# Attention pieces between expert steps: transposes together, scores with states, one run of outputs

## The chip, the cores and the metric

The kernel runs on one core of one Trainium2 chip. The metric is the device time in microseconds (us) of one execution, taken as the median of several runs. The engines are PE (TensorE, matmuls), DVE (VectorE), ACT (ScalarE), POOL (GpSimd) and SP (SyncE, which here only issues DMAs).

## What is computed

A linear attention with a complex, decaying state feeds a mixture of eight experts whose gate is balanced by eight rounds of row and column normalization. Cut to what matters:

```python
# q, k, v, a_re, a_im: (4, 8, 768, 48)
for t in range(S):
    S_re, S_im = ar * S_re - ai * S_im, ar * S_im + ai * S_re   # a, scaled to |a| <= 0.999
    S_re = S_re + k[:, :, t] (outer) v[:, :, t]
    y[:, :, t] = q[:, :, t] @ S_re
x = y as (3072, 384)
P = exp(x @ w_gate - max); eight times: rows to 1, columns to N / E
for e in range(8):
    out += P[:, e:e+1] * (relu(x @ w1[e]) @ w2[e])
```

## The kernel before

The kernel has two phases. Phase 1 computes the attention and, between its parts, the first two experts. Phase 2 computes the other six experts for all tokens and is not touched.

Phase 1 cuts the 3072 tokens into 12 blocks of 256 (`SUB`), three for each of the four sequences, and each block into two chunks of 128 (`CH`). For a block, `elem(i)` (line 295) makes the cumulative products of `a` and from them scaled keys `kh` and queries `z`, almost all on DVE; this is called the chain of the block here. `mix(i)` (line 427) is the attention proper. It is a generator: what stands between two `yield`s is a piece. For each chunk it issues 12 DMAs on SP that copy keys and queries by heads into `ks` and `qs` (lines 437 to 441; two buffers of each, taken in turn by chunk), and then uses four helpers, each for a half `g` of the eight heads:

- `keys(g)`: four PE transposes of `ks` (L460) and an ACT copy to `kt` (L462)
- `scores(g)`: four PE products of `ks` and `qs` (L474; fp32 products show as two instructions each) and a masked copy on DVE into `sc` (L477)
- `state(g)`: four PE products of `kt` and `v` into `U` (L469)
- `outs(g)`: 16 or 32 small PE products into `xp` (L491), of masked scores with `v` and, unless the chunk is the first of its sequence, of `qs` with the state of the chunk before

The last chunk of a sequence has no keys and no states. After a chunk's states the state is carried on by five DVE operations (L517 to L528). After the outputs, `xh` (L530, ACT) and `xl` (L531, DVE) split the result into a high and a low part for the experts. The transposes and the scores share one PSUM pool of two buffers (tag `s`), `U` and `xp` have one buffer each, and `kt` and `sc` have two.

An expert step (`experts`, line 147) for one of the 16 hidden tiles of the two experts runs six PE matmuls of the second layer for a tile three steps back (L158 to L160) and nine of the first layer (L179 to L181), then two ACT operations and one on DVE (`hl`, L187). A plain step is these 15 matmuls.

For block 0, `phase1` (line 190) runs the pieces of `mix(0)` one after another and after each calls twice the loader of the last weight tiles (`load_thirds`, line 132). For each later block `i` it runs the 16 steps of block `i - 1` and, from step `LEAD` on (11 for block 1, 10, 8, 6 for blocks 2 to 4, then 4), one piece of `mix(i)` after each; the pieces that are left then run in a row.

PE's order is that of the program text (`manual_schedule`). The orders of DVE, ACT and SP are laid out by a planner that simulates the program with a model of the durations; on the chip each engine then follows its order. Three places in it are pinned: `behind` holds both masks of block 0's second chunk and the first mask of block 1 behind certain operations of the next chain.

Before, a chunk has five pieces: transposes and scores of half 0; states of half 0 and transposes of half 1; outputs of half 0 and scores of half 1; states of half 1; outputs of half 1 with all that follows them.

Of the kernel before, what the change touches and what calls it, by code (L numbers as in the profile page):

```python
# [20 lines left out]
NCH = SUB // CH  # L21
# [22 lines left out]
def slot(h):  # L44
    return (h % 4) * 128 + (h // 4) * 80


def piece(h, b):
    q = (h % 4) * 128
    if h < 4:  # L50
        return slice(q + 32 * b, q + 32 * b + 32)
    return slice(q + 96 - 32 * b, q + 128 - 32 * b)


class Net:
# [134 lines left out]
    def phase1(self, c1, ca):  # L190
# [41 lines left out]
        for i in range(ns):  # L232
            mix = self.mix(i)
            if i == 0:
                n = 0
                while True:
                    with tc.issue_after(self.act0.ins), tc.issue_after(self.dve0.ins):
                        if next(mix, self) is self:
                            break
                    with tc.issue_after(self.act0.ins):  # L240
                        for _ in range(2):
                            if late and next(late[0], self) is self:
                                late.pop(0)
                                next(late[0], None) if late else None
                    n += 1
                for g in late:
                    for _ in g:
                        pass
                with tc.issue_after(self.gl.ins):
                    self.elem(1)  # L250
                self.behind(0, 1, 0, k=1)
                self.behind(0, 1, 1, k=3)
                continue
            lg = self.logits(i - 1)
            for n in range(2 * NF):
                self.moe.send((i - 1, n // NF, n % NF))
                if n in (1, 2):
                    next(lg)
                if n >= LEAD.get(i, 4):
                    next(mix, None)  # L260
# [166 lines left out]
    def mix(self, i):  # L427
# [6 lines left out]
        for c in range(NCH):  # L434
# [17 lines left out]
            def keys(g, i=i, c=c, ks=ks, kts=kts, lastc=lastc):  # L452
                if lastc:
                    return
                if i == 0:
                    kt_p = self.psB.tile([128, 4, SK], F32, tag="po", name=f"ktp{i}_{c}_{g}")
                else:
                    kt_p = self.psS.tile([128, 4, SK], F32, tag="s", name=f"ktp{i}_{c}_{g}")
                for j in range(4):
                    nc.tensor.transpose(kt_p[:, j, :], ks[:, 4 * g + j, :], self.ident[:SK, :SK])  # L460
                kts[g] = tmp.tile([128, 4, SK], F32, tag="kt", name=f"kt{i}_{c}_{g}", bufs=2)
                self.kt = nc.scalar.activation(kts[g], kt_p, AF.Copy)  # L462

            def state(g, c=c, U=U, kts=kts, lastc=lastc):
                if lastc:
                    return
                for j in range(4):
                    h = 4 * g + j
                    nc.tensor.matmul(U[:, h, :], kts[g][:, j, :], vt[:, c, slot(h):slot(h) + D], start=True, stop=True)  # L469

            def scores(g, i=i, c=c, ks=ks, qs=qs, sss=sss):
                sp = self.psS.tile([128, 4, CH], F32, tag="s", name=f"sp{i}_{c}_{g}")
                for j in range(4):
                    nc.tensor.matmul(sp[:, j, :], ks[:, 4 * g + j, :], qs[:, 4 * g + j, :CH], start=True, stop=True)  # L474
                ss = sss[g] = self.sc[self.isc]
                self.isc = 1 - self.isc
                self.masks[i, c, g] = nc.vector.copy_predicated(ss, self.mask, sp)  # L477

            def outs(g, c=c, xp=xp, qs=qs, sss=sss, S0=S0, first=first):
                for b in range(2):  # L480
                    for inter in range(1 if first else 2):
                        for j in range(4):
                            h = 4 * g + j
                            q = 32 * j
                            o = xp[q:q + 32, 2 if b else g, :]
                            pc = piece(h, b)
                            lw = S0[:, pc] if inter else vt[:, c, pc]
                            rw = qs[:, h, :CH] if inter else sss[g][:, j, :]
                            st = g == 0 and b == 0 and inter == 0
                            sp_ = g == 1 and b == 1 and (first or inter == 1)  # L490
                            nc.tensor.matmul(o, lw, rw, start=st, stop=sp_, tile_position=(0, q), skip_group_check=True)  # L491

            keys(0)
            scores(0)
            yield
            state(0)
            keys(1)
            yield
            outs(0)
            scores(1)  # L500
            yield
            state(1)
            if not lastc:
                with self.tc.issue_after(self.kt.ins):
                    nc.scalar.activation(rr[0:D], R[0:D], AF.Copy)
                    nc.scalar.activation(rr[64:64 + D], R[0:D], AF.Copy)
                    nc.scalar.activation(rn[0:D], R[64:64 + D], AF.Copy, scale=-1.0)
            yield
            outs(1)
            if not lastc:  # L510
                sh = [SK, 2, H // 2, D]
# [20 lines left out]
            if c == NCH - 1:  # L532
                for a, t in ((0, xh), (1, xl)):
                    nc.sync.dma_start(self.x_d[i // NS][:, i % NS, a], t.bitcast(F32).rearrange("p c (j t) -> p c j t", t=CH))
            yield

    def logits(self, i):
        nc = self.nc
# [483 lines left out]
```

## Time and profile before

| what | us |
|---|---|
| median of 3 runs (1840.32 to 1843.8) | 1842.44 |
| span of the profiled execution | 1839.6 |
| PE busy in the span | 1774.3 |
| DVE busy | 1361.8 |
| ACT busy | 734.3 |
| PE busy from 0 to 92 us (block 0 and the first steps) | 68.95 |
| PE busy from 92 to 308 us (216 us) | 196.31 |
| DVE busy from 92 to 308 us | 191.22 |
| PE busy from 617 to 1839 us (1222 us, after the attention) | 1200.08 |

The span runs from the first to the last instruction of the profiled execution. The page gives no other time of that execution; the runs were timed apart. PE's matmuls overlap, so the busy time of a group is more than the time by which it moves what follows; for that, the starts of matmuls one after the other are read. "Idle before" and "waited for" tell what released an engine after it stood still. The granted clock is the share of full speed at which TensorE ran.

### The profile page before, as it was taken

What the parts mean: (1) busy time and instruction counts of PE and PEld (TensorE: products, weight loads), DVE (VectorE), ACT (ScalarE), POOL (GpSimd) and SP (SyncE); (2) the same over time, 40 slices, a digit from 0 to 9 for tenths busy, and PEclk for the clock granted to TensorE, in tenths of its full rate; (3) what the DMA queues carried; (4) which work ended last, traced back from release to release, by engine and by line L of the source; (5) the groups of instructions that cost most, each with busy time, mean ns of one, the idle gap of its engine ahead of it and who ended that gap; (6) DMA issues with size and microseconds to landing.
All of it is one profiled execution on the core that took longest, in us unless ns stands there. A gap on an engine that the chain in (4) does not pass through costs nothing.

```text
span 1839.6 us, 30590 instructions
## 1 busy us (share of the span) xinstructions
PE 1774.3 (96%) x12024; PEld 1731.9 (94%) x12024; DVE 1361.8 (74%) x3060; ACT 734.3 (40%) x1597; POOL 6.4 (0%) x15
## 2 busy tenths in 40 slices
PE   5979999999999999999999999999999999999998
PEld 3869999999999989899999999998999999999998
DVE  7888989888883586967676767687776767575754
ACT  7534444445443443424242424343433333242421
POOL 1000000000000000000000000000000000000000
PEclk9979999999999999999999999999999999999999
DMA  6333433333332430401010101123220101020100
GB/s 209 96 104 88 132 113 110 116 111 111 118 97 73 147 112 4 150 20 52 18 52 18 52 18 52 49 96 97 69 86 18 52 5 65 1 69 1 52 24 31
DMA packets 120632, 132.83 MB, mean 72 GB/s; under 512 B 9632, under 2 KB 100512, under 8 KB 120480
## 3 DMA queue, kind: packets, MB, share of 16 engines
q1 hardware_dynamic: 119680, 130.41, 23.0%
q8 instruction: 96, 1.57, 0.4%
q14 instruction: 56, 0.46, 0.1%
q10 hardware_dynamic: 800, 0.39, 0.1%
HBM read 88.22 MB, written 23.59 MB: 61 GB/s over the span
## 4 chain that ended last, share of the span: by engine, by line
PE 82%; DVE 9%; DMA 4%; ACT 2%; issue 1%; SPq 1%; DVEq 0%; ACTq 0%
PE po L747 10%; PE po L745 10%; PE po L746 10%; PE P L784 9%; PE P L785 9%; PE P L786 9%; PE po L158 3%; PE ph L180 3%; PE ph L181 3%; PE ph L179 3%; PE po L160 3%; PE po L159 3%; PE sp L474 2%; PE y L491 2%; DMA raw<-in_w_dram 2%; PE U L469 1%
## 5 line engine op out<-in xcount | busy, mean ns | idle before, releaser
L747 PE MATMUL po<-wc,hl 128*128 128x384 f32 x1152 | 385.3, 334 | 3.1 <-DVE hl L806 3.1
L745 PE MATMUL po<-wc,hh 128*128 128x384 f32 x1152 | 385.0, 334 | 0.0
L746 PE MATMUL po<-wc,hh 128*128 128x384 f32 x1152 | 384.8, 334 | 0.0
L805 ACT ACTIVATE hh<-c 128x384 fp32r<-128x384 f32 x384 | 200.9, 524 | 322.2 <-DVE c L794 320.9
L806 DVE SCALAR_TENSOR_TENSOR hl<-c,hh 128x384 fp32r<-128x384 f32 x384 | 211.9, 552 | 66.5 <-ACT hh L805 58.5
L747 PEld LDWEIGHTS po<-wc,hl 128*128 128x128 f32 x1152 | 216.2, 188 | 4.4 <-DVE hl L806 4.4
L745 PEld LDWEIGHTS po<-wc,hh 128*128 128x128 f32 x1152 | 216.2, 188 | 0.4 <-ACT hh L805 0.4
L746 PEld LDWEIGHTS po<-wc,hh 128*128 128x128 f32 x1152 | 216.2, 188 | 0.0
L799 ACT ACTIVATE s<-P 128x384 f32<-128x384 f32 x192 | 94.1, 490 | 270.8 <-PE P L786 270.8
L185 ACT ACTIVATE hh<-ph 128x256 fp32r<-128x256 f32 x192 | 73.3, 382 | 243.7 <-PE ph L181 243.0
L180 PE MATMUL ph<-xl,w 128*128 128x256 f32 x576 | 162.8, 283 | 5.4 <-DVE xl L531 5.4
L179 PE MATMUL ph<-xh,w 128*128 128x256 f32 x576 | 162.2, 282 | 0.6 <-ACT xh L530 0.6
L181 PE MATMUL ph<-xh,w 128*128 128x256 f32 x576 | 162.4, 282 | 0.0
L784 PE MATMUL P<-B,wa 128*128 128x384 f32 x480 | 160.7, 335 | 0.9 <-DVE c L794 0.6
L786 PE MATMUL P<-B,wa 128*128 128x384 f32 x480 | 160.4, 334 | 0.0
L785 PE MATMUL P<-B,wa 128*128 128x384 f32 x480 | 160.4, 334 | 0.0
L158 PE MATMUL po<-w,hh 128*128 128x384 f32 x384 | 141.2, 368 | 1.2 <-ACT yst L163 1.2
L160 PE MATMUL po<-w,hl 128*128 128x384 f32 x384 | 130.7, 340 | 0.0
L159 PE MATMUL po<-w,hh 128*128 128x384 f32 x384 | 130.3, 339 | 0.0
L794 DVE TENSOR_TENSOR c<-P,u 128x384 f32<-128x384 f32 x192 | 106.2, 553 | 31.2 <-PE P L786 29.9
L794 DVE TENSOR_TENSOR u<-u,s 128x384 f32<-128x384 f32 x96 | 53.3, 555 | 100.9 <-ACT s L799 100.9
L187 DVE TENSOR_TENSOR hl<-hf,hh 128x256 fp32r<-128x256 f32 x192 | 80.4, 419 | 48.1 <-ACT hf L186 47.3
(188 smaller groups left out, 3665.4 us busy)
## 6 DMA issues: line engine op xcount, KB each, us to landing
raw<-in_w_dram SPq DMA_DIRECT2D x48, 768.0 KB, 4.3
qs<-z SPq DMA_DIRECT2D x144, 64.5 KB, 2.6
qk<-in_aqk_dram SPq DMA_DIRECT2D x12, 768.0 KB, 4.9
ks<-kh SPq DMA_DIRECT2D x144, 64.0 KB, 2.6
ye_d<-yst SPq DMA_DIRECT2D x48, 192.0 KB, 2.1
y<-ye_d SPq DMA_DIRECT2D x48, 192.0 KB, 2.4
z<-in_aqk_dram SPq DMA_DIRECT2D x11, 768.0 KB, 7.0
B<-x_d SPq DMA_DIRECT2D x40, 192.0 KB, 3.6
```

Source lines behind the costliest of these rows:

```text
L158: nc.tensor.matmul(po[k], hh[:, s], w2h, start=f == 0, stop=False)
L179: nc.tensor.matmul(ph, w[:, 0, cs], xh[:, ct, :], start=(ct == 0), stop=False)
L180: nc.tensor.matmul(ph, w[:, 0, cs], xl[:, ct, :], start=False, stop=False)
L181: nc.tensor.matmul(ph, w[:, 1, cs], xh[:, ct, :], start=False, stop=(ct == NCT - 1))
L745: nc.tensor.matmul(po[k], hh[:, s], w2[:, 0, i], start=first, stop=False)
L746: nc.tensor.matmul(po[k], hh[:, s], w2[:, 1, i], start=False, stop=False)
L747: nc.tensor.matmul(po[k], hl[:, s], w2[:, 0, i], start=False, stop=last)
L784: nc.tensor.matmul(ps, t[:, 0, k], x[:, 0], start=first, stop=False)
L785: nc.tensor.matmul(ps, t[:, 0, k], x[:, 1], start=False, stop=False)
L786: nc.tensor.matmul(ps, t[:, 1, k], x[:, 0], start=False, stop=last)
L805: A.activation(hh, c, AF.Relu)
L806: V.scalar_tensor_tensor(hl, c, 0.0, hh.bitcast(F32), ALU.max, ALU.subtract)
```

## The change

The same helpers are called in another grouping. A chunk's pieces are now: both halves' transposes; both halves' scores, then both halves' states; an empty piece (not for block 0); both halves' outputs with all that follows. In blocks after the first, no `yield` stands after the first chunk's outputs, so the second chunk's copies and transposes belong to the same piece. A block has seven pieces in place of ten; block 0 has six. For a chunk with states, the distance from scores to outputs is two expert steps, as it was.

```diff
             keys(0)
-            scores(0)
-            yield
-            state(0)
             keys(1)
             yield
-            outs(0)
+            scores(0)
             scores(1)
-            yield
+            state(0)
             state(1)
             if not lastc:
                 with self.tc.issue_after(self.kt.ins):
                     nc.scalar.activation(rr[0:D], R[0:D], AF.Copy)
                     nc.scalar.activation(rr[64:64 + D], R[0:D], AF.Copy)
                     nc.scalar.activation(rn[0:D], R[64:64 + D], AF.Copy, scale=-1.0)
             yield
+            if i:
+                yield
+            outs(0)
             outs(1)
             if not lastc:
...
             if c == NCH - 1:
                 for a, t in ((0, xh), (1, xl)):
                     nc.sync.dma_start(self.x_d[i // NS][:, i % NS, a], t.bitcast(F32).rearrange("p c (j t) -> p c j t", t=CH))
-            yield
+            if i == 0 or c == NCH - 1:
+                yield
```

## The prediction

> **What bounds the kernel now.** I read the page first, for its span.
>
> ```profile
> span 1839.6 us, 30590 instructions
> ```
>
> The page gives nothing of the profiled execution beyond its span of 1839.6 us. The median of the runs shown is 1842.4, so some 2.8 us lie around the span; the change touches nothing there, and I add every microsecond found in the span to the median one for one. Then I read the windows: the end of block 0's attention, the slowest slice, two short slow stretches, and the even part of the attention phase.
>
> ```profile
> 57.00:68.00 11.00, 8.59 (x116) 7.37 (x114) 10.76 (x29) 4.32 (x13) 0.00 (x0) 1.00 0.63 175
> 92.00:138.00 46.00, 33.74 (x304) 30.79 (x303) 41.32 (x92) 16.91 (x38) 0.00 (x0) 0.80 0.35 104
> 123.00:133.00 10.00, 9.20 (x86) 7.87 (x87) 7.23 (x11) 6.43 (x10) 0.00 (x0) 0.50 0.13 33
> 181.00:191.00 10.00, 8.02 (x79) 6.77 (x80) 9.93 (x16) 1.00 (x2) 0.00 (x0) 0.50 0.29 72
> 308.00:617.00 309.00, 309.00 (x2913) 297.93 (x2912) 235.45 (x546) 140.06 (x364) 0.00 (x0) 1.00 0.34 102
> ```
>
> The columns are length, busy PE, PEld, DVE, ACT, POOL, granted clock, DMA share. From 308 to 617 us PE is never idle: there only a change in what PE itself runs can count. From 92 to 138 us it is idle for 12.3 us (46.00 less 33.74), and it runs two stretches of 10 us at half clock. PE's waits between 94 and 245 us:
>
> ```profile
> PE y L491 <- DVE sc L477: 7.1, 5, 2.9
> PE ktp L460 <- DMA ks<-kh: 4.8, 1, 4.8
> PE sp L474 <- DMA qs<-z: 3.2, 1, 3.2
> PE ph L180 <- DVE xl L531: 3.0, 2, 1.8
> ```
>
> So the attention phase has two parts. In blocks 1 to 3 pieces run close behind one another and PE waits for the masked scores (sc), for a query copy (qs) and for the low halves (xl). From block 4 on it is PE alone. After 617 us nothing that the change touches runs.
>
> **The change, even part first.** It adds and removes no instruction. PE's order is that of the program, so PE does what the diff says; ACT, DVE and SP are ordered anew by the planner. What changes on PE is how often it passes from expert matmuls to attention matmuls and back. The timeline of PE in an even stretch (start, length, count at the end):
>
> ```profile
> 413.14 0.55 PE L460 MATMUL ktp<-ident,ks 112*128 112x112 f32 x4
> 413.52 1.07 PE L474 MATMUL sp<-qs,ks 112*128 112x128 f32 x8
> 414.35 0.42 PE L158 MATMUL po<-w,hh 128*128 128x384 f32 x1
> 414.61 0.34 PE L159 MATMUL po<-w,hh 128*128 128x384 f32 x1
> ...
> 419.71 0.28 PE L181 MATMUL ph<-xh,w 128*128 128x256 f32 x1
> 419.92 0.42 PE L491 MATMUL y<-sc,v 128*32 128x128 f32 x8
> ...
> 420.94 1.16 PE L474 MATMUL sp<-qs,ks 112*128 112x128 f32 x8
> 421.86 0.42 PE L158 MATMUL po<-w,hh 128*128 128x384 f32 x1
> ...
> 430.31 0.34 PE L158 MATMUL po<-w,hh 128*128 128x384 f32 x1
> 430.49 0.34 PE L159 MATMUL po<-w,hh 128*128 128x384 f32 x1
> ...
> 432.43 0.34 PE L158 MATMUL po<-w,hh 128*128 128x384 f32 x1
> ```
>
> I read from start to start. A step with no piece takes 2.12 us (430.31 to 432.43). The first expert matmul after attention work takes 0.26 (414.35 to 414.61), a plain one 0.18 (430.31 to 430.49): 0.08 for each return. Entry into a run of outputs costs 0.09 (419.71 to 419.92 is 0.21; the L181 matmuls beside it follow at 0.12). Four transposes take 0.38, a half's scores 0.83, but 0.92 behind outputs (420.94 to 421.86), and a half's outputs 1.02.
>
> Before, a chunk has five returns, two entries into outputs and one score run behind outputs. After, it has three returns; in a block's first chunk the outputs run on into the next chunk's transposes, which makes it two. Mean saving for a chunk: 2.5 returns x 0.08 + one entry 0.09 + one slow score run 0.09 = 0.38, plus a little inside the longer runs, which I bound at 0.1 and take at 0.05. That is 0.43. Blocks 4 to 11 have 16 chunks, so **7 us** (6 to 9). Nothing covers this: PE is busy all the time there.
>
> Two groups of PE whose lengths are needed next (count, then busy us and mean ns), from the view of groups by line with shapes kept apart:
>
> ```profile
> L469 PE MATMUL U<-v,kt 128*112 128x48 f32 x320 | 37.5, 262 | 1.0 <-ACT kt L462 0.9
> ...
> L143 PE MATMUL wd<-wr,ident 128*128 128x256 f32 x24 | 8.6, 452 | 0.0
> ```
>
> The state products are 40 runs of 8 in 37.5 us, 0.94 each; less the tail of the last matmul, which for the transposes is 0.55 busy against 0.38 from start to start, I count 0.77, so both halves 1.5 and scores with states 3.2.
>
> What waits could replace it? Both masks are now needed at the head of one run of outputs, with the next expert step queued behind it. But two whole steps (4.2 us) and both state products lie between scores and outputs, and both masks need 1.5 us (below). The two transpose copies on ACT are needed a step and 1.7 us of scores after the transposes. The other chunk's 12 copies into ks and qs move past two steps and past the waiting SP queue, each about 0.63 us of issue; only the loads of block i+2 stand behind them, and they get earlier.
>
> **Block 0** has six pieces where it had ten. With two calls of the weight loader at each, three of the twelve thirds of weight tiles slip behind the last outputs: a quarter of L143's 8.6 us is 2.2, and with the third matmul of each 3.2 at most. The 4.76 us wait at the head of block 1 (next fence) hides them; without that cover they cost up to 3.2. I take nothing.
>
> **Block 1** begins when its keys land and ends at the first expert matmul after its last outputs:
>
> ```profile
> 98.65 0.67 PE L460 MATMUL ktp<-ident,ks 112*128 112x112 f32 x4 [4.76 <-DMA ks<-kh]
> ...
> 131.00 0.69 PE L158 MATMUL po<-w,hh 128*128 128x384 f32 x1
> ```
>
> Its start is set by block 1's own chain on DVE, which the change does not shorten, so 98.65 stays. Before, all of chunk 1 runs in a row after the 16th step: 5 pieces one behind the other, each needing the one before through ACT or DVE. After, only one run of outputs is left there. Worked forward: 8 transposes and a step, 0.76 + 2.2 at full clock and some 4.8 with most of it at half, to 103.4 (the 3.2 us wait for qs falls into that step); scores and states 3.2 to 106.6; two steps 4.4 to 111.0; outputs and the next 8 transposes 2.7 to 113.7; a step 2.2 to 115.9; scores and states 3.2 to 119.1; outputs 2.0 to 121. That is **10 us** before 131.0. No half-clock stretch follows if no long wait is left, which is worth up to 2 us more in block 2's first steps. Unknown is how late the masks come. Nearest rows, block 2:
>
> ```profile
> 177.58 1.06 PE L474 MATMUL sp<-qs,ks 112*128 112x128 f32 x8
> 181.51 0.66 PE L491 MATMUL y<-sc,v 128*32 128x128 f32 x8 [2.88 <-DVE sc L477]
> ...
> 188.79 0.69 PE L158 MATMUL po<-w,hh 128*128 128x384 f32 x1
> ```
> ```profile
> 180.74 0.72 DVE L477 COPY_PREDICATED sc<-mask,sp 128x512 f32<-128x512 uint8 x1
> ```
>
> A mask takes 0.72 and began some 2.2 us after its scores (177.58 + 0.9 to 180.74), since DVE was in block 3's chain. In the new block 1 the states (1.4) cover most of that: 0 to 2 us left, plus up to 5 if that wait slows the clock. I take 0.
>
> **Block 2** has no keys or states in its chunk 1. Before, scores, outputs, scores, outputs in a row took from 177.58 to 188.79, 11.2 us. After, scores go out a step before, and 2.0 us of outputs remain; with the steps counted as above, block 2 is **8 us** shorter. So PE would enter block 3 some 20 us early. There the chain of DVE and SP caps it:
>
> ```profile
> 144.07 3.76 SPq L441 DMA_DIRECT2D qs<-z  x6
> ...
> 191.35 0.55 SPq L441 DMA_DIRECT2D qs<-z  x1
> ```
> ```profile
> qs<-z SPq DMA_DIRECT2D x144, 64.5 KB, 2.6
> ```
>
> The last qs copies of blocks 2 and 3 are issued by 147.8 and 191.4 and land 2.6 us later at the median, about 150 and 194. Block 2's scores would want theirs at 151: just in time. Block 3's would want theirs at 192.6: about 2 late, so I take 18 in place of 20. Block 3 itself loses waits of about 2 us (its last pieces also end a step earlier, which frees the second xl wait, 3.0 - 1.8 = 1.2, and smaller ones) and some crossings: 2.5.
>
> **Sum:** 18 + 2.5 + 7 = 27.5. I take 1.5 off for the mask wait that stays somewhere in blocks 1 and 2: 26 us, so 1842.4 - 26 = **1816.4**.
>
> **A rule weighed.** The half-clock stretch from 123 begins beside a 2.0 us wait for sc and the one from 181 beside the 2.88 us wait. The Trainium skill, "TensorE: Matmul & The Clock Gate", table in "Why this matters for your kernels", has the clock fall only after idle gaps of over about 3 us. By that rule these waits were too short to cause it. The rows speak for shorter gaps, since both stretches stand at such waits and the even part, without waits, has a mean clock of 1.00. What it would mean if the waits were not the cause is the third rival.
>
> **Rivals.**
> 1. *DVE takes the early gain back.* DVE is busy 41.32 of 46 us at 92 to 138; masks and low halves that come earlier delay the chains of blocks 2 and 3, and PE waits for ks and qs there. For it: that busy share, and block 2's qs just in time. Against: part of DVE's idle time is waiting for PE. If half of the 20.5 is lost, the gain is 10 + 7, less 2 for the clock: 15, so 1827; at worst the even part alone, 1835.
> 2. *Even more.* All waits, and half-clock time, go, and the last attention work stands three steps further from the end of phase 1 (ten pieces end 3 later than seven), 3 x 2.12 = 6 us sooner for the loads of phase 2: 27.5 + 2 + up to 6 = 36, so 1806.
> 3. *Slower: the attention runs themselves drop the clock.* The place is blocks 4 to 10, where runs without an expert step grow from 2.0 us to 3.1 (scores with states) and 2.7 (outputs with transposes). For it: both slow stretches lie in attention-only work, and the page's rule leaves the waits out as cause. Against: from 57 to 68 us PE runs mostly attention and the clock is 1.00. A slow stretch of 10 us loses 5 us. Over 5 of them eat the 26; one in each of 8 blocks gives 41 - 26 = 15 slower, 1857.
> 4. *No change:* the time won returns as waits at block 3's chain and at the start of the last phase; 1842.
>
> **Chances.** The forecast (1808 to 1824) 0.58, rival 1 0.22, rival 2 0.08, rival 3 0.07, rival 4 0.05. A difference under about 0.2% (3.7 us) can't be told from no change. Faster 0.88, same 0.05, slower 0.07. The range reaches from rival 2's end to rival 1's, 1804 to 1833; rivals 3 and 4 and the tails, about 0.18, are left out.
>
> **What would show it.** In the profile after: PE's wait for sc in blocks 1 to 3 falls from 7.1 us to under 2; no window at clock 0.50 after 110; block 1's last outputs end near 121, block 3's transposes start near 192; in the even part the time for two chunks and their steps falls by 0.9. It is wrong if PE waits for ks or qs in block 2 or 3 for more than 4 us in all, if hl or xl shows among PE's waits after 308, or if the clock after 308 is under 1.00.

## The result and the profile after

The changed kernel takes 1808.4 us (median of 4 runs, 1806.8 to 1810.7) against 1841.5 us before: a ratio of 0.9814, 95% interval 0.9803 to 0.9826. It is faster by 33 us, where 26 were forecast (1842.4 to 1816.4). The page of the changed kernel, span and first line of busy times:

```profile
span 1806.7 us, 30538 instructions
...
PE 1756.0 (97%) x12024; PEld 1725.3 (95%) x12024; DVE 1361.6 (75%) x3060; ACT 730.1 (40%) x1597; POOL 6.4 (0%) x15
```

The span is 32.9 us shorter, with the same instructions on PE and the same DVE time. The windows that answer to those of before (length, busy PE, PEld, DVE, ACT, POOL, clock, DMA share):

```profile
92.00:138.00 46.00, 39.62 (x382) 38.26 (x381) 41.84 (x96) 19.62 (x50) 0.00 (x0) 0.93 0.39 116
104.00:126.00 22.00, 19.71 (x257) 18.86 (x256) 20.99 (x64) 6.57 (x17) 0.00 (x0) 1.00 0.49 139
308.00:581.00 273.00, 273.00 (x2578) 267.58 (x2580) 226.42 (x524) 128.68 (x339) 0.00 (x0) 1.00 0.37 109
```

PE is idle for 6.4 us from 92 to 138 where it was 12.3, and after 103.7 no half-clock stretch is left in the attention phase, where before three of them, 23.9 us in all, lay between 122.9 and 191.2. All of PE's waits from 94 to 245 us:

```profile
PE ktp L460 <- DMA ks<-kh: 3.7, 1, 3.7
PE ph L180 <- DVE xl L531: 3.4, 3, 2.3
PE lt L550 <- ACT ls L546: 0.4, 1, 0.4
```

The waits for the masked scores (7.1 us before) and for qs (3.2) are gone; those for keys and for low halves stay. Block 1 in the timeline of PE:

```profile
98.41 1.73 PE L460 MATMUL ktp<-ident,ks 112*128 112x112 f32 x8 [3.66 <-DMA ks<-kh]
...
116.28 1.95 PE L474 MATMUL sp<-qs,ks 112*128 112x128 f32 x16
118.07 1.68 PE L469 MATMUL U<-v,kt 128*112 128x48 f32 x16
119.68 0.43 PE L491 MATMUL y<-sc,v 128*32 128x128 f32 x8
...
121.59 0.44 PE L158 MATMUL po<-w,hh 128*128 128x384 f32 x1
...
125.33 0.39 PE L180 MATMUL ph<-xl,w 128*128 128x256 f32 x1 [2.29 <-DVE xl L531]
```

The last outputs follow the states without a gap, and the next step's first matmul starts at 121.59 (131.00 before, 121 by the prediction's sum).

To see where the 32.9 us come from, the starts of equal instructions are compared. The gate products of block k (L542 before) run in the second expert step of that block, after its attention. The lead of the changed kernel over the old one, in us, with that of the experiments below (one trace of each; a negative lead is a delay; P is the first matmul of phase 2, L784 before):

| kernel | block 0 | 1 | 2 | 3 | 4 | 5 | 7 | 11 | P | end |
|---|---|---|---|---|---|---|---|---|---|---|
| before, start at | 72.2 | 139.9 | 194.2 | 244.6 | 294.3 | 340.4 | 436.7 | 622.8 | 663.6 | 1839.6 |
| changed | -0.9 | 11.4 | 18.4 | 21.3 | 23.2 | 23.8 | 25.6 | 28.5 | 31.0 | 32.9 |
| e1_early | -2.5 | 8.1 | 15.0 | 18.0 | 13.1 | 13.0 | 13.2 | 13.2 | 13.6 | 14.1 |
| e13_early4 | -0.5 | 10.5 | 17.5 | 20.5 | 22.4 | 19.7 | 19.7 | 19.7 | 20.0 | 20.2 |
| e2_even | -1.7 | -1.7 | -1.9 | -1.5 | -0.5 | 0.2 | 1.9 | 4.0 | 6.4 | 2.7 |
| e3_old_order | -0.9 | 4.4 | 8.3 | 11.3 | 12.4 | 12.2 | 11.3 | 5.5 | 8.0 | 6.6 |
| e4_no_empty | -0.9 | 10.7 | 18.8 | 22.4 | 23.4 | 19.5 | 17.6 | 19.9 | 22.4 | 22.1 |
| e5_late11 | -1.9 | 9.5 | 16.9 | 19.9 | 21.8 | 22.5 | 24.2 | 27.2 | 27.5 | 29.1 |
| e6_lead12 | -0.4 | 10.4 | 13.5 | 16.9 | 17.9 | 13.8 | 15.5 | 18.4 | 20.9 | 21.8 |
| e8_lead13 | -2.2 | 15.0 | 14.6 | 18.3 | 19.3 | 17.2 | 18.9 | 21.8 | 24.3 | 24.6 |
| e9_lead12_short | 0.5 | 14.2 | 13.6 | 17.2 | 18.2 | 15.5 | 17.2 | 20.1 | 22.6 | 25.1 |
| e7_split | -1.3 | 7.6 | 13.8 | 15.3 | 17.1 | 16.4 | 17.8 | 20.6 | 22.7 | 22.4 |
| e11_leads_short | -1.4 | 15.7 | 18.1 | 19.9 | 21.4 | 22.1 | 21.9 | 24.8 | 27.3 | 27.2 |
| e12_leads | -0.7 | 16.6 | 20.1 | 21.9 | 23.4 | 24.0 | 23.9 | 26.8 | 29.4 | 27.6 |

In the changed kernel blocks 1 to 3 bring 21.3, blocks 4 to 11 another 7.2, the passage into phase 2 2.5, and phase 2 itself 1.9. The even part, block 10 in the timeline of PE:

```profile
508.99 0.34 PE L158 MATMUL po<-w,hh 128*128 128x384 f32 x1
...
511.10 0.93 PE L460 MATMUL ktp<-ident,ks 112*128 112x112 f32 x8
511.80 0.42 PE L158 MATMUL po<-w,hh 128*128 128x384 f32 x1
...
536.16 0.44 PE L158 MATMUL po<-w,hh 128*128 128x384 f32 x1
```

From 508.99 to 536.16 lie seven steps and two chunks: 27.17 less 7 x 2.12 is 12.33 us of attention. Before, two chunks and ten steps of block 7 took 34.26 us (393.82 to 428.08), so 13.06 of attention. That is 0.73 a block, 0.37 a chunk; the prediction had 0.43.

### The profile page after: what moved, and what is told of

Its sections match the earlier page's. It is cut to its first block, busy times and chain, and to the rows that moved or that the text cites. A ratio compares the mean times of both kernels' runs of the same rounds, so it can differ in the third digit from the quotient of the medians.

```text
span 1806.7 us, 30538 instructions
## 1 busy us (share of the span) xinstructions
PE 1756.0 (97%) x12024; PEld 1725.3 (95%) x12024; DVE 1361.6 (75%) x3060; ACT 730.1 (40%) x1597; POOL 6.4 (0%) x15
## 5 line engine op out<-in xcount | busy, mean ns | idle before, releaser
L800 ACT ACTIVATE s<-P 128x384 f32<-128x384 f32 x192 | 94.1, 490 | 278.6 <-PE P L787 278.5
L158 PE MATMUL po<-w,hh 128*128 128x384 f32 x384 | 136.3, 355 | 0.0
L159 PE MATMUL po<-w,hh 128*128 128x384 f32 x384 | 129.3, 337 | 0.0
L180 PEld LDWEIGHTS ph<-xl,w 128*128 128x128 f32 x576 | 108.9, 189 | 4.4 <-DVE xl L531 4.4
```

The costliest lines, as they stand in the source:

```text
L180: nc.tensor.matmul(ph, w[:, 0, cs], xl[:, ct, :], start=False, stop=False)
```

## The experiments

Each run is compared with runs of the kernel before on the same chip; medians of before were 1843.8 to 1844.8 there.

**Early blocks or late ones.** `e1_early` has the new grouping in blocks 1 to 3 alone, `e2_even` from block 4 on:

```diff
+            new = 1 <= i <= 3      # e1_early; e2_even: i >= 4; e13_early4: 1 <= i <= 4
             keys(0)
-            keys(1)
-            yield
-            scores(0)
-            scores(1)
...
+            if new:
+                (the pieces of the change)
+            else:
+                (the five pieces of before)
```

> New grouping in blocks 1 to 3 alone, the old five pieces a chunk everywhere else. If the early gain stands by itself, the experts' steps of block 3 begin some 21 us earlier than before, as they do in the changed kernel (244.6 to 223.4), and that lead is kept to the end: about 1820. If it only lives because later blocks are also shorter (the chains of blocks 4 on would then catch PE), part of it is lost after block 3 and the time is over 1826.

> New grouping from block 4 on alone, blocks 0 to 3 as before. Crossings theory: 0.7 to 0.9 us a block, 6 in all; and if the last phase profits from the attention that ends three steps earlier, another 2 to 4 between the last block's gate products and the end: 1831 to 1833. If the late gain comes only from phase 1 being early as a whole, 1836.

`e1_early`: 1827.1 us, ratio 0.9905 (0.9874 to 0.9937), in its second range. `e2_even`: 1838.4 us, 0.9969 (0.9957 to 0.9980), later than either of its two. The two gains in the traces, 14.1 and 2.7, do not add up to 32.9. In `e1_early` the lead at block 3 is 18.0, which with its late start (2.5) is nearly what the change has; then 5 us are lost at block 4 and nothing after. All of PE's waits from 260 to 600 us in `e1_early`:

```profile
PE ph L180 <- DVE xl L544: 3.9, 1, 3.9
```

Block 4 there has its ten old pieces, which end right before the next block's first step, and that step waits for the low halves. `e2_even` gains 5.6 us from block 3 to block 11 (-1.5 to 4.0), 2.4 in the passage to phase 2 as the change does, and then loses 3.7 in phase 2. So its crossings and its passage came as expected, and the miss is the loss in phase 2, which neither range foresaw.

**One block more.**

> New grouping in blocks 1 to 4, old pieces elsewhere. In the run with blocks 1 to 3 the lead of 18 us fell by 5 at the end of block 4, where PE waited 3.9 us for the low halves. If that was block 4's own ten pieces ending right before the next block's first step, it goes: block 5's gate products come at about 318 to 320 (with blocks 1 to 3: 327.4) and the time is 1819 to 1823. If it was the DVE chain catching up with PE, the same loss appears one block later, and the time is 1825 to 1828.

1822.5 us, 0.9884 (0.9859 to 0.9908): within the first range. The loss at block 4 is gone (22.4). But 2.7 us are lost one block later, where the lead meets the chain. PE's waits in `e13_early4` from 260 to 600 us:

```profile
PE sp L474 <- DMA qs<-z: 2.4, 1, 2.4
```

So both readings held in part. The changed kernel passes the same place without a wait, by little. Its SP queue, and then PE at block 5:

```profile
274.53 5.06 SPq L441 DMA_DIRECT2D qs<-z  x6
```
```profile
281.80 1.39 PE L474 MATMUL sp<-qs,ks 112*128 112x128 f32 x11
```

The last of these six copies lands at 281.6 in the trace, and the first score starts at 281.8. In the new grouping the scores stand a step behind the first transposes, here 2.9 us (278.88 to 281.80), where before they followed at once (302.04 to 302.43); the change needs its queries that much later after its keys.

**Order or number of pieces.** `e3_old_order` keeps the old order of the calls and joins pieces (six in a block); `e8_lead13` keeps the new grouping and begins block 1 two steps later, so that four pieces stand in a row:

```diff
 # e3_old_order
             keys(0); scores(0); yield
-            state(0); keys(1); yield
-            outs(0); scores(1); yield
-            state(1); (rr, rn); yield
-            outs(1)
+            state(0); keys(1); outs(0); scores(1); yield
+            state(1); (rr, rn); outs(1)
 # e8_lead13
-LEAD = {1: 11, 2: 10, 3: 8, 4: 6}
+LEAD = {1: 13, 2: 10, 3: 8, 4: 6}
```

> The old order of the calls (transposes and scores of a half, its states, its outputs, then the other half), but cut into six pieces a block after block 0. Theory room: what counts is how few pieces are left in a row after the sixteenth step; then blocks 1 to 3 gain nearly as with the change, 15 to 20 us, and the whole is 1812 to 1820. Theory grouping: what counts is that both halves' scores go out together with the states as cover; then the masks are waited for in each chunk, and the time is over 1828.

> The change, with block 1 begun two steps later, at 13, so that four of its seven pieces stand in a row after the sixteenth step, nearly as many as the five before. Theory room: the row costs what it cost before, the gate products of block 1 come at 134 or later (128.5 with the change, 139.9 before). Theory grouping: in the new grouping a row waits little, since the states cover the masks; they come by 131.

`e3_old_order`: 1834.7 us, 0.9946 (0.9932 to 0.9961), between the two ranges. Its six pieces leave one in a row after block 1's sixteenth step, where the change has two, one of them empty. Joining pieces in the old order is worth about half: blocks 1 to 3 win 12.2 (from -0.9 to 11.3) where the change wins 22.1, and block 1 wins 5.3 where the change wins 12.3. PE's waits from 94 to 460 us in it:

```profile
PE ktp L460 <- DMA ks<-kh: 4.7, 1, 4.7
PE y L491 <- DVE sc L477: 4.4, 5, 2.1
PE ph L180 <- DVE xl L533: 3.2, 2, 2.3
PE sp L474 <- DMA qs<-z: 3.0, 1, 3.0
```

Only 0.8 us of the mask waits lie in blocks 1 to 3, against 7.1 before: so fewer pieces in a row remove most of the mask waits of these blocks by themselves. What the old order keeps in block 1 is the wait of 3.0 us for the queries, since its first scores follow the transposes at once; the step between them covers it in the change. With it come a wait for keys that is 1.0 longer and two half-clock stretches, 10.2 us from 96.6 and 3.4 from 130.8, where the change has one of 6.8. The other large mask waits stand at 402 and 451 us (1.2 and 2.1), where a half's outputs follow its scores after one step, and the second has 6.8 us at half clock behind it. The one step alone is not the reason: `e4_no_empty` below has one step too, in the new grouping, and no mask wait.

In `e8_lead13` block 1 wins 17.2 (-2.2 to 15.0), more than with the change, with four pieces in a row. Its timeline in that row:

```profile
113.38 2.05 PE L474 MATMUL sp<-qs,ks 112*128 112x128 f32 x16 [0.31 <-ACT kt L462]
115.27 1.68 PE L469 MATMUL U<-v,kt 128*112 128x48 f32 x16
116.89 0.43 PE L491 MATMUL y<-sc,v 128*32 128x128 f32 x8
```

Outputs start behind the states without a wait, with no step between: with both halves' scores together and the states behind them, a row of pieces costs nothing here. (Part of the 17.2 is the later start: PE runs two more steps where the change waits 3.66 us for keys, and the clock is 1.00 from 65.6 to 147.5.) So for the masks of block 1 either is enough, few pieces in a row or the new grouping, and the two theories don't exclude each other. The whole kernel is slower than the change all the same, 1815.1 us, 0.9847 (0.9828 to 0.9866): at block 2 it waits 2.5 us for keys and has 6.8 us of half clock behind that, and the next group shows the like.

**Where the cap lies.** Five kernels begin pieces at other places: `e4_no_empty` and the two begun at 12, and later the two with all early blocks begun later.

```diff
 # e4_no_empty (the change without its empty piece)
-            if i:
-                yield
 # e6_lead12; e9_lead12_short also has "if i > 1 or i and c:" for "if i:"
+LEAD = {1: 12, 2: 10, 3: 8, 4: 6}
 # e12_leads; e11_leads_short also has "if i > 2 or i and c:" for "if i:"
+LEAD = {1: 13, 2: 11, 3: 9, 4: 8, 5: 8, 6: 6}
```

> The change without its empty piece: one step in place of two between scores and outputs. A step and the states are 3.6 us; masks that come 2.2 us after their scores and need 1.5 are then ready just about in time, so waits only where there are no states (blocks 2, 5, 8, 11, some 1 us each): 1807 to 1812. If the masks are usually later than that, PE waits in most of 24 chunks, 15 us or more: over 1822.

> The change, with block 1's pieces begun one step later, at 12. That step fills 2.1 us of the 3.7 us wait for the keys; three pieces in place of two are left in a row. If a row of scores, states and outputs waits for its masks (2 to 3 us, and perhaps half clock after), the gate products of block 1 come no earlier than 128.5, or up to 3 later. If states cover the masks in a row as well, they come 2 earlier.

> Begun at 12 as in the run beside it, and without the empty piece in block 1's first chunk, so that again one run of outputs alone is left after the sixteenth step. The wait at 98.4 falls to about 1.6 us; the gate products of block 1 come 2 to 4 us earlier than 128.5. At block 5 the queries land at 281.6 and are used at 281.8 in the changed kernel: if the chain is the cap there, these 2 to 4 us come back as a wait for keys or queries in block 5 and the time is 1807 to 1809; if not, 1804 to 1806.

`e4_no_empty`: 1818.9 us, 0.9860 (0.9830 to 0.9891). `e6_lead12`: 1818.3 us, 0.9863 (0.9844 to 0.9882). `e9_lead12_short`: 1817.4 us, 0.9862 (0.9843 to 0.9882). None met its range for the whole. In `e4_no_empty` PE never waits for a mask, with one step between scores and outputs, and is as early as the change up to block 4; then it waits elsewhere (94 to 460 us):

```profile
PE ktp L460 <- DMA ks<-kh: 6.6, 2, 3.8
PE ph L180 <- DVE xl L529: 2.6, 1, 2.6
PE po L158 <- ACT yst L163: 2.3, 3, 1.8
```

The second wait for keys, 2.8 us, is block 5's; the 1.8 us for yst stand at 403, with 3.4 us at half clock behind them. In these three kernels and `e8_lead13` the chain of block 5 ends later than with the change: at 278.6 in `e4_no_empty`, 283.4 in `e6_lead12`, 281.9 in `e8_lead13`, 283.0 in `e9_lead12_short`, against 273.7. That is not a cause by itself: in all but `e4_no_empty` PE too is 3.0 to 4.4 us behind the change at block 3, and what DVE does for PE is late with it. `e6_lead12` had its gate products of block 1 at 129.5, as the first half of its expectation says. `e9_lead12_short` was 14.2 us ahead at block 1, as expected, and won nothing more at block 2, where it waits 2.3 us for the queries and has 6.8 us of half clock behind that. One source of the late chain is seen on DVE. Its waits in `e6_lead12` from 96 to 146 us, while it works on block 2's chain:

```profile
DVE hl L187 <- ACT hf L186: 5.5, 3, 2.9
DVE x L410 <- ACT sq L409: 2.2, 1, 2.2
DVE x L391 <- ACT sq L390: 2.1, 1, 2.1
```

and in the changed kernel from 96 to 141:

```profile
DVE hl L187 <- ACT hf L186: 1.8, 1, 1.8
DVE x L391 <- ACT sq L390: 1.7, 1, 1.7
```

The planner put low halves of expert tiles (hl) in front of chain operations before their inputs from ACT were there, and DVE stood 9.8 us in place of 3.5, 5.5 and 1.8 of it for hl; block 2's chain ends at 146.6 there, at 140.8 in the changed kernel. Why the planner's order differs so much between these builds was not tried.

The losses can be counted. From block 0's gate products to block 11's, PE is idle for 7.6 us in the changed kernel, 12.2 in `e4_no_empty`, 12.6 in `e6_lead12` and 13.0 in `e9_lead12_short`. Half of PE's busy time at half clock, an estimate of what the clock costs, is 2.6, 6.2, 8.2 and 6.7. What is left is 511.0 to 511.5 us in all four, so idle time and slow clock are the whole loss.

> The change with blocks begun later (13, 11, 9, 8, 8, 6 for blocks 1 to 6) and no empty piece in the first chunk of blocks 1 and 2. Chain theory: after block 1 the chains of blocks 2 to 5 on DVE are the cap; starting the pieces later lets PE do expert steps in place of waiting for keys, so the waits for keys and queries at blocks 2 and 5 go and the 3.6 us won at block 1 in the run begun at 13 are kept: 1801 to 1806. If the later ends bring waits for the low halves in their place, 1808 to 1814.

> The same later starts with the empty pieces kept, so one more piece stands in a row in blocks 1 and 2. Chain theory: as the run beside it, within 3 us of it, 1802 to 1808. If rows without states wait for masks, 2 to 4 us more are lost at the end of block 2.

`e11_leads_short`: 1814.4 us, 0.9842 (0.9817 to 0.9867). `e12_leads`: 1813.4 us, 0.9834 (0.9812 to 0.9856). Both keep 4 to 5 us more than the change at block 1 (15.7 and 16.6 against 11.4). `e11_leads_short` has given it back at block 2 (18.1 against 18.4), `e12_leads` by block 5 (24.0 against 23.8). PE's waits in `e12_leads` from 94 to 400 us, the three largest:

```profile
PE ph L180 <- DVE xl L531: 4.3, 3, 1.7
PE sp L474 <- DMA qs<-z: 2.7, 2, 1.6
PE sp L474 <- ACT hf L186: 0.9, 1, 0.9
```

The waits move from keys to low halves and queries, 7.0 us in the first two rows. The expected 1801 to 1808 was missed (1814.4 is also just over the 1808 to 1814 that waits for low halves were given), and no version has a lower ratio than the change. Of the 5.3 us by which the trace of `e12_leads` ends behind the change's, 1.6 are lost before phase 2 and 3.6 in phase 2, of which more below; so the later starts themselves neither win nor lose much.

**The join of the two pieces, and the end.** `e7_split` keeps a yield after the first chunk's outputs; `e5_late11` begins block 11 at step 7.

```diff
 # e7_split
-            if i == 0 or c == NCH - 1:
-                yield
+            yield
 # e5_late11
+LEAD = {1: 11, 2: 10, 3: 8, 4: 6, 11: 7}
```

> The change with a yield kept after each first chunk's outputs, so that outputs and the next chunk's transposes stand in two pieces (eight pieces a block). Crossings theory: one more return to the experts a block, 0.08 to 0.15 us each, 1 to 2 us over all; the attention of each block ends a step later, still early enough for blocks 5 on: 1808 to 1811. If the ends of blocks matter more (one more piece is left in a row in blocks 1 and 2), 2 to 4 us are lost there: over 1811.

> The change, with the last block's pieces begun at step 7 in place of 4, so that its attention ends as close to phase 2 as it did before. Joint theory: the 2.4 us that the changed kernel gains between the last block's gate products and the first check transpose come from the three steps that attention ends earlier; they go, and PE waits again for the stored expert tile and the check: 1810 to 1812. If they come from another order of the planner there, the time stays at 1808.

`e7_split`: 1818.9 us, 0.9864 (0.9843 to 0.9885). From block 5 on it loses under 0.1 us a block against the change; 7 us are lost before, at the ends of blocks 1 to 5, with 5.9 us of waits for low halves in three places up to 320 us (3.4 in the change). So the second range held, with more than the 2 to 4 us lost that it named, but the row is not what costs in block 1: its last outputs let go of PE at 121.81, 0.2 us after the change's 121.59. Then PE waits 3.3 us for the low halves where the change waits 2.3, and runs at half clock from 125.9 to 132.7; together that is most of what block 1 loses. Why the low halves come later there is open.

`e5_late11`: 1812.3 us, 0.9826 (0.9804 to 0.9849). The interval overlaps the change's, so the traces have to decide. In its trace it runs 1.3 us behind the change from block 3 to block 11 (1.1 of them from the start), then falls back by 2.2 more before phase 2. PE's waits in it from 585 to 640 us:

```profile
PE po L158 <- ACT yst L163: 1.5, 1, 1.5
PE okp L568 <- DVE ok L565: 0.3, 1, 0.3
PE cp L601 <- DVE cs L597: 0.3, 1, 0.3
```

In the changed kernel only the last of these remains there. So most of the 2.5 us at the passage comes from attention that ends three steps earlier. The other traces sort the same way: the passage brings 2.2 to 2.5 us in the ten kernels whose block 11 has six to eight pieces begun at step 4, and 0.3 to 0.4 in the three where it has ten or begins later (`e1_early`, `e13_early4`, `e5_late11`).

## Why the prediction was right, and where it was off

The direction held, and so did the parts that the sum had for blocks 1 to 3 and the even part; the size was 26 us by the sum and 32.9 in the traces. The measured 1808.4 stands at the lower edge of the forecast's 1808 to 1824, nearer to the second rival's 1806 than to 1816.4. The difference has five parts: 2.5 (the passage), 1.9 (phase 2), 1.5 (the mask wait), 0.8 (blocks 1 to 3: 21.3 for 20.5) and 0.2 (the even part).

- **"After 617 us nothing that the change touches runs"** is the step that failed. 2.5 us came in the passage into phase 2, which the sum had at nothing and only the second rival named, and 1.9 us in phase 2 itself. The 2.5 are explained by `e5_late11`. The 1.9 are not: between the builds of this study phase 2 took from 2.5 us less to 3.7 us more than before, without a change in its code. Part of that is the clock. At 641 and 643 the changed kernel waits 1.15 and 0.61 us for hl, as before did at 672 and 674 (1.14 and 0.61), but only in the changed kernel is the clock 0.50 behind it, from 643.0 to 646.4; `e2_even`, `e7_split`, `e11_leads_short` and `e12_leads` have two such stretches in phase 2. The rest stays open.
- **1.5 us off for a mask wait that stays** was not needed: no mask is waited for in blocks 1 to 3. Of the bound of 0 to 2 us with up to 5 for the clock, the lower end came true.
- **Block 1**, 10 us: 9.4, and 2.0 more in block 2's first steps, as said. The step at half clock ended at 103.7 (sum: 103.4), the outputs started at 119.7 (119.1).
- **Block 2**, 8 us: 7.0. The 18 us at block 3's start came out as 18.4 (first transposes at 192.06 in place of 210.43), but by luck: the cap that was named was not there. The queries of block 3 landed at 190.6, 3 us earlier than the rows of before had led me to think, and its scores started at 195.0 unhindered. PE was 18.4 early because 9.4, 2.0 and 7.0 us came for 10, 2 and 8. The chain came within 0.2 us of being the cap two blocks later.
- **Block 3**, 2.5: 2.9. **Even part**, 7: 7.2, with 0.37 a chunk where 0.43 was taken and the rows gave 0.38; block 4 added 1.9, of which 0.6 is a wait for low halves that PE had before between 245 and 308 us and has no longer.
- **Block 0**, nothing: its gate products come 0.9 us later, and the wait for block 1's keys hides that (3.66 in place of 4.76; the keys start at 98.41).
- **First rival** (DVE takes the gain back): not in the changed kernel, where PE waits for no keys and no queries after block 1's. Waits for them are back at later blocks in seven of the experiments (`e4_no_empty`, `e6_lead12`, `e8_lead13`, `e9_lead12_short`, `e11_leads_short`, `e12_leads`, `e13_early4`), so the risk was real.
- **Third rival** (attention runs drop the clock): refuted by the windows of the changed kernel, 1.00 from 104 to 126 and from 308 to 581, with runs of up to 3.3 us of attention without a step.
- **The signs**: those for blocks 1 to 3 came (no wait for masks, 121.59, 192.06). Taken by the word, two signs against it came too, both in phase 2 and not in the attention: PE waits 3.0 us for hl there, but 3.1 before, and the clock is 0.50 from 643.0 to 646.4.
- **The clock** is a term that the sum carried mostly unseen. It counted two slow stretches of 10 us, where the trace has 6.8 (from 99.0), 10.2, 3.4 and 10.2. It names "up to 2 us more" for those that go, but its lengths for after are at full clock and stand against rows of before that ran at half clock in part: the 11.2 us of block 2 reach from 177.58 to 188.79, the slow stretch from 180.9 to 191.2. From block 0's gate products to block 3's, before and after:

```profile
72.20:244.64 172.44, 153.44 (x1314) 145.72 (x1312) 151.62 (x355) 76.09 (x187) 0.00 (x0) 0.91 0.33 96
```
```profile
73.06:223.39 150.33, 142.78 (x1314) 138.54 (x1312) 134.09 (x317) 74.13 (x186) 0.00 (x0) 0.98 0.35 105
```

That is 22.1 us shorter. PE's idle time falls from 19.0 to 7.6, by 11.4 us. Its half-clock time falls from 30.7 to 6.8 us; half of PE's busy time in it, an estimate of its cost, falls from 12.3 to 2.6, by 9.7. So of the early gain nearly as much is the clock as the waits, and 1.0 is left for the crossings.

On the rule of the Trainium skill that was weighed ("TensorE: Matmul & The Clock Gate", "Why this matters for your kernels": gaps of over about 3 us bring the clock down), the runs speak against a fixed length. After a wait of 2.3 us at the same place the clock stayed in `e1_early` and fell in `e5_late11`, windows of both:

```profile
129.00:132.00 3.00, 3.00 (x25) 2.96 (x24) 2.94 (x6) 2.09 (x5) 0.00 (x0) 1.00 0.35 139
```
```profile
127.00:130.00 3.00, 3.00 (x13) 3.00 (x13) 2.00 (x4) 2.35 (x5) 0.00 (x0) 0.50 0.16 64
```

So waits as short as the 2.0 and 2.9 us of before can be the cause. No run changed a wait alone; what the traces show together stands in the last section.

## What to carry to other kernels

Where small dependent pieces are laid between steps of other work, put the operations that need the same helper engine side by side and let work that needs no result of it (here the state products) run behind them: a row of pieces then ran without a wait for masks. Fewer pieces in the old order removed most of these waits too, but kept the one for the queries, and won about half in blocks 1 to 3. When a wait goes, look at the granted clock behind it: here the slow stretches were worth nearly as much as the waits. Count how early a producer chain on another engine is at each block before counting on a lead: in `e13_early4` 2.7 us were given back where the queries came late. And when a part of the kernel ends earlier, look at what its end releases, the first loads and buffers of the next part, even if no instruction there is changed.

## What was not expected of the hardware

The granted clock halves after waits of PE of about 2 us in some places and not in others: 2.29 us at 125 in the changed kernel left it at 1.00, 2.33 us at 126 in `e5_late11` brought 0.50 for about 3 us, and in `e4_no_empty` a wait of 1.8 us at 403 was followed by 0.50 as well. In each trace the clock changes on a grid of 3.41 us, so the slow stretches last 3.4, 6.8, 10.2 us or more such steps. Where a wait falls in that grid is what differs. The windows of the grid around the waits, in the changed kernel and in `e5_late11`:

```profile
120.73:124.14 3.41, 2.31 (x43) 1.85 (x31) 3.41 (x8) 0.49 (x1) 0.00 (x0) 1.00 0.50 129
124.14:127.55 3.41, 2.22 (x15) 2.22 (x16) 3.35 (x8) 2.15 (x3) 0.00 (x0) 1.00 0.66 261
```
```profile
123.39:126.80 3.41, 1.10 (x9) 1.10 (x10) 3.38 (x9) 1.49 (x1) 0.00 (x0) 1.00 0.71 269
```

The changed kernel's wait is cut in two, and PE is idle for 1.10 and 1.19 us in the two windows; that of `e5_late11` lies in one, with 2.31 us idle. Counted over the fourteen traces, from the first fall of the clock to 20 us before the end: of the windows at full clock with over 1.8 us of idle PE all 44 were followed by 0.50, of those with under 1.4 us one of 7012, and of those between 13 of 33. Of the windows at half clock, 72 of the 82 with under 0.37 us of idle PE were followed by full clock, and none of the 43 with more. This is counted, not tried: no run moved a wait in the grid. By it the changed kernel had some luck at 125 us, where the same wait in one window would have cost it a stretch at half clock, as in `e5_late11`.
